# One block of x^T by five transposing transfers of 128 columns instead of one of 640

## The chip, the cores and the metric

The kernel runs on one core of one Trainium2 chip. The metric is the device time of one execution in microseconds; the runs before the change took 182.01, 182.14 and 183.18 us, median 182.14 us. Engine names are those of the profile: PE is TensorE (PEld its weight loads), DVE is VectorE, ACT is ScalarE, POOL is GpSimd, and SP is SyncE, which here only issues DMA transfers (SPq is its queue).

## The reference

Two linear-attention blocks A and B work on the same input x (1 x 2048 x 640, bf16), and a gate made from x mixes their outputs. H is 32, so a head has 20 columns.

```python
def block(x, wqkv, wo):                       # called for A and for B
    qkv = split(x @ wqkv)                     # q, k, v: 32 heads of 20 columns
    phi = lambda t: where(t > 0, t + 1, exp(t)) + 1e-6
    pq, pk = phi(q), phi(k)
    kv = einsum("bhsd,bhse->bhde", pk, v)
    z = pk summed over s
    num = einsum("bhqd,bhde->bhqe", pq, kv)
    den = einsum("bhqd,bhd->bhq", pq, z)[..., None] + 1e-6
    return merge_heads(num / den) @ wo
g = sigmoid((x * gate_w).sum(-1, keepdims=True))
out = g * block(x, A_wqkv, A_wo) + (1 - g) * block(x, B_wqkv, B_wo)
```

## The kernel before

The products x @ wq and x @ wk contract over the 640 columns of x, so TensorE needs x with its columns on the partitions. This is the tile xT, 128 partitions x 5 column groups x 2048 rows: `xT[:, c, s]` holds column 128c + p of row s. A column group c is one step of a contraction; five of them make one product. The rows come in 16 chunks of 128 (D0 to D15 in the plan) and in four blocks of 512.

The first block is filled in two ways: chunks 0 and 1 are transposed by TensorE (`x_transpose`, L290), and rows 256 to 511 by one transposing transfer from DRAM. The second, third and fourth block are each filled by one transposing transfer of 512 rows x 640 columns (L221 and L222), from `load_xT` (L205). All transposing transfers are issued by SP, which works its list strictly in order: first parts of x and of wk of block A, then the half block of xT, then wq of block A in three transfers (L220), then the three blocks of xT, then x in its own layout into the tile xn (L1311 and L1313), then wv (L1230) and wo (L1237, L1240) of block A, and after that wk of block B, which waits for TensorE to be done with wk of block A.

The order of TensorE's, VectorE's and ScalarE's work is written out by hand in the string FIRST (L32 to L50); the engines take the names in that order. For the change this stretch of it matters:

```
... E.P1 ... U0.n0 D2.top D4.c0 D4.c1 E.p1s E.P2 D4.c2 D4.c3 D3.clamp D3.lift0 tq3 sq03 U0.exp0 U0.lift0 tq1
D3.top D3.gl sq01 D4.c4 E.exp0 tq2 D4.exp0 U0.n1 D4.gl sq02 E.clamp D4.clamp D7 ... D6 ... Q00.P5 Q00.P6 ... D5.c0
```

- E.P1 and E.P2 (class `QPair`, L748) are 4 and 6 matmuls of q on block 1 of the rows, 512 columns of output each; E.p1s (L758) is ScalarE's copy of the state between them, so E.P2 waits for that copy. U0.n0 and U0.n1 (class `Fifth`, L388) are 5 matmuls each of the last fifth of q, n0 on the first block of rows, n1 on the second.
- D4 is the first chunk of the second block. D4.c0 to D4.c4 (class `KFirst`, L732, through `k_mm`, L338) are its five column groups, two matmuls of 320 columns each; D4.cN reads column group N of the second block and no other. D5, D6 and D7 are the other chunks of that block, D8 to D11 those of the third, D12 to D15 those of the fourth.
- sq03, sq01, sq02, sq04 (`sq_sum`, L421) are sums and differences of blocks of xT on VectorE. sq03 reads column groups 0 and 1 of the first two blocks, sq01 column groups 0 to 3 of the second.
- tq1 to tq4 (L429) are differences of parts of wq on VectorE, D3.top, D4.clamp, E.clamp and their like VectorE's part of phi, and the names with exp, lift and gl are ScalarE's.

A reader of a tile waits for the transfer that wrote the part it reads. With one transfer for a block, everything that reads any column group of the block waits for the same completion.

Of the kernel before, what the change touches and what calls it, by code (L numbers as in the profile page):

```python
# [9 lines left out]
P = 128  # L10
# [7 lines left out]
DT = D // P  # L18
ST = S // P
NB = 4  # L20
CB = 4
HB = 512
# [56 lines left out]
def kernel(  # L79
# [11 lines left out]
    nc = tc.nc  # L91
    x2 = A_x.flatten_outer_dims()
# [43 lines left out]
    xT = persist.tile([P, DT, S], BF16, name="xT")  # L136
# [62 lines left out]
    def load_x(eng, lo, hi):  # L199
        eng.dma_start(out=xn[:, lo:hi, :], in_=xb0[:, lo:hi, :])  # L200

    def load_wk(eng, lo, hi):
        eng.dma_start(out=wk[0][:, lo:hi, 0:D], in_=wq_dram[0][:, lo:hi, D:2 * D])

    def load_xT(lo, hi):  # L205
        nc.sync.dma_start_transpose(out=xT[:, :, lo:hi], in_=x2[lo:hi, :])

    wq[0] = wpool.tile([P, DT, D], BF16, tag="wq", name="wqA")
    with tc.manual_schedule():
        load_x(nc.sync, 0, 1)  # L210
        load_x(nc.scalar, 1, 2)
        load_wk(nc.sync, 0, 1)
        load_wk(nc.scalar, 1, 2)
        nc.scalar.dma_start(out=g5[:], in_=gate_w.rearrange("(c p) -> c p", p=P))
        load_wk(nc.sync, 2, 3)
        load_wk(nc.sync, 3, DT)
        load_xT(HB // 2, HB)
        nc.scalar.preload_act_table_set("natural_log_exp_and_others")
        for lo, hi in ((0, 2), (2, 4), (4, DT)):
            nc.sync.dma_start(out=wq[0][:, lo:hi, :], in_=wq_dram[0][:, lo:hi, 0:D])  # L220
        for n in range(1, NB):  # L221
            load_xT(n * HB, (n + 1) * HB)  # L222


# [1 line left out]
    for r in range(4):  # L226
# [3 lines left out]
        out=spread[:].rearrange("p (h t) -> p h t", t=TW), in_=I4[:, :, None].to_broadcast([P, H, TW])  # L230
    )
    for lo in range(0, HF, K6):
        part = maskE[:, lo:min(lo + K6, HF)]
        for sign, base in ((1, 0), (-1, Dh - 1)):
            nc.gpsimd.affine_select(
                out=part, in_=part, pattern=[[-sign * Dh, part.shape[1] // Dh], [0, Dh]],
# [3 lines left out]
    for rows, n in ((slice(0, 2 * H), H // 2), (slice(2 * H, P), H)):  # L240
        nc.gpsimd.tensor_copy(
            out=E4_rows[rows, 0:n], in_=I4[rows, 0:n, None].to_broadcast([rows.stop - rows.start, n, Dh])
# [1066 lines left out]
    with tc.manual_schedule():  # L1309
        pts = k_first()  # L1310
        nc.sync.dma_start(out=xn[:, 2:CB, :], in_=xb0[:, 2:CB, :])  # L1311
        for n in range(1, NB):
            nc.sync.dma_start(  # L1313
                out=xn[:, n * CB:(n + 1) * CB, :], in_=x2[n * HB:(n + 1) * HB, :].rearrange("(q p) d -> p q d", p=P)
# [4 lines left out]
        lo, hi = GT  # L1319
# [320 lines left out]
```

## Time and profile before

| | |
|---|---|
| runs, us | 182.01, 182.14, 183.18; median 182.14 |
| the profiled execution's own time, us | 182.23 |
| its span from first to last instruction, us | 180.5 |
| granted TensorE clock | 0.998 |
| DVE busy / ACT busy, us | 151.2 (84%) / 112.4 (62%) |
| DMA packets / MB | 22514 / 19.18 |

A busy share is the time in which an engine works, divided by the span. A row of a timeline gives the start, the duration over the whole group, the engine, the line of the code, the operation, what is written and what is read, and the count; brackets at its end give the idle time of the engine ahead of it and what ended that. A DMA issue's row is the time that the issuing queue spent on it, not the time in which the data moved.

### The profile page before, as it was taken

Reading aid. Unit: us, or ns where it says so; the run is one execution under the profiler, and the core shown is the slowest. Engines: PE = TensorE matmul, PEld = TensorE weight load, DVE = VectorE, ACT = ScalarE, POOL = GpSimd, SP = SyncE. Lnnn points to the kernel's source line nnn. Section 1 sums busy time; section 2 is a strip of 40 time slices with the busy share of each in tenths; the row PEclk is TensorE's granted clock in tenths of the full one; section 3 lists DMA queues with packets and bytes.
Section 4 is the critical chain, followed back from the end, with each engine's and each line's share of the span. In section 5 each row is a group of like instructions: output and inputs, shape, how many; then the busy total and the mean of one; then the engine's idle time right before and its main releaser. Section 6 shows DMA issues by size and latency. Waiting matters only on the chain.

```text
span 180.5 us, 3357 instructions
## 1 busy us (share of the span) xinstructions
PE 176.0 (97%) x1266; PEld 116.8 (65%) x1266; DVE 151.2 (84%) x283; ACT 112.4 (62%) x235; POOL 4.4 (2%) x19
## 2 busy tenths in 40 slices
PE   8989999999999999999999999999999999999993
PEld 3646666665666577566656675766678777777772
DVE  1379999999999996888999997987988979686773
ACT  2387978999763444587778676774715756456410
POOL 7100000000000000000000000000000000000000
PEclk9999999999999999999999999999999999999999
DMA  5999999205046024000000023134902550223133
GB/s 180 309 207 169 237 362 293 66 4 182 0 116 184 5 74 162 0 0 0 2 4 0 2 56 129 44 115 133 252 5 65 150 152 0 84 103 111 73 113 109
DMA packets 22514, 19.18 MB, mean 106 GB/s; under 512 B 10210, under 2 KB 21986, under 8 KB 22498
## 3 DMA queue, kind: packets, MB, share of 16 engines
q1 hardware_dynamic: 21912, 18.47, 37.1%
q10 hardware_dynamic: 586, 0.49, 0.8%
q8 instruction: 10, 0.16, 0.4%
q14 instruction: 6, 0.05, 0.1%
HBM read 11.86 MB, written 4.80 MB: 92 GB/s over the span
## 4 chain that ended last, share of the span: by engine, by line
PE 90%; DMA 4%; SPq 3%; DVE 1%; issue 0%
PE q L522 16%; PE kA L338 9%; PE kB L338 9%; PE gs L840 9%; PE gs L1329 9%; PE oy L1124 6%; PE oz L1124 5%; PE ox L1124 5%; DMA xT<-in_A_x_dram 4%; PE ow L1124 4%; PE kB L522 3%; PE gB L810 2%; PE gA L810 2%; PE qA L388 2%; PE qB L388 1%; PE q L388 1%
## 5 line engine op out<-in xcount | busy, mean ns | idle before, releaser
L338 PEld LDWEIGHTS <-xT 128*128 128x128 bf16 x280 | 27.2, 98 | 15.9 <-DMA xT<-in_A_x_dram 1.1
L338 PE MATMUL kA<-wkA,xT 128*128 128x320 bf16 (+1 forms) x160 | 24.1, 301 | 0.6 <-DMA xT<-in_A_x_dram 0.6
L552 DVE TENSOR_SCALAR e<-e 128x640 bf16<-128x640 bf16 (+2 forms) x59 | 19.1, 334 | 4.6 <-ACT e L546 4.3
L546 ACT ACTIVATE e<-q 128x512 bf16<-128x512 f32 x32 | 18.5, 598 | 5.7 <-PE q L522 5.2
L338 PE MATMUL kB<-wkB,xT 128*128 128x320 bf16 x120 | 19.2, 299 | 0.0
L546 ACT ACTIVATE e<-kB 128x640 bf16<-128x640 f32 (+1 forms) x18 | 11.4, 647 | 7.3 <-PE kB L522 3.2
L546 ACT ACTIVATE e<-kA 128x640 bf16<-128x640 f32 x16 | 11.4, 713 | 4.6 <-PE kA L338 3.9
L528 DVE TENSOR_TENSOR q<-q,p 128x512 f32<-128x512 f32 x16 | 11.1, 695 | 1.7 <-PE q L522 1.2
L559 DVE SCALAR_TENSOR_TENSOR pk<-kB,e 128x640 bf16<-128x640 f32 (+1 forms) x16 | 11.6, 736 | 0.4
L1124 PEld LDWEIGHTS <-xT 128*128 128x128 bf16 x85 | 8.1, 98 | 2.9
L1124 PEld LDWEIGHTS <-pqTA 128*128 128x128 bf16 x85 | 8.1, 98 | 2.8
L1124 PEld LDWEIGHTS <-pqTB 128*128 128x128 bf16 x80 | 7.8, 98 | 3.0
L522 PE MATMUL q<-xT,wqB 128*128 128x512 bf16 x32 | 9.7, 379 | 0.0
L1129 DVE TENSOR_TENSOR osb<-oz,u 128x320 bf16<-128x320 f32 (+2 forms) x18 | 7.9, 452 | 1.9 <-PE oz L1124 1.6
L1187 ACT COPY u<-ox 128x320 f32<-128x320 f32 x8 | 3.4, 426 | 9.4 <-PE ox L1124 9.4
L522 PE MATMUL q<-SQ,TM 128*128 128x512 bf16 x32 | 8.5, 379 | 0.0
L1329 PEld LDWEIGHTS <-xn 128*128 128x128 bf16 x64 | 6.1, 98 | 3.1 <-issue 0.7
L810 PEld LDWEIGHTS <-xn 128*128 128x128 bf16 x64 | 6.3, 98 | 2.8
L840 PEld LDWEIGHTS <-xn 128*128 128x128 bf16 x64 | 6.1, 98 | 2.9 <-issue 0.7
L559 DVE SCALAR_TENSOR_TENSOR pk<-kA,e 128x640 bf16<-128x640 f32 x8 | 6.6, 820 | 0.4
L559 DVE SCALAR_TENSOR_TENSOR pqTB<-q,e 128x512 bf16<-128x512 f32 x10 | 6.8, 683 | 0.0
L1124 PE MATMUL oz<-MB,xT 128*128 128x320 bf16 (+2 forms) x45 | 6.8, 284 | 0.0
(205 smaller groups left out, 373.6 us busy)
## 6 DMA issues: line engine op xcount, KB each, us to landing
out_dram<-osb SPq DMA_DIRECT2D x14, 160.0 KB, 1.8
xn<-in_A_x_dram SPq DMA_DIRECT2D x3, 640.0 KB, 7.8
wvA<-in_A_wqkv_dram SPq DMA_DIRECT2D x1, 800.0 KB, 11.0
wkB<-in_B_wqkv_dram SPq DMA_DIRECT2D x1, 800.0 KB, 4.5
wqB<-in_B_wqkv_dram SPq DMA_DIRECT2D x1, 800.0 KB
wvB<-in_B_wqkv_dram SPq DMA_DIRECT2D x1, 800.0 KB
MA<-m_rows SPq DMA_DIRECT2D x1, 800.0 KB, 4.6
MB<-m_rows SPq DMA_DIRECT2D x2, 400.0 KB, 4.4
```

The lines of the kernel that those rows point to most:

```text
L338: nc.tensor.matmul(pt[:, hf, 0:n], lhsT=xT[:, c, i * P:(i + 1) * P], rhs=wk[b][:, c, hf * HF:hf * HF + n], start=(c == 0), stop=(c == DT - 1),
L388: nc.tensor.matmul(dst, lhsT=mixed(wq[b][:, c, :], m), rhs=xT[:, c, n * HB:(n + 1) * HB], start=first, stop=last,)
L522: nc.tensor.matmul(dst, lhsT=left(c), rhs=right(c), start=first and k == 0, stop=last and k == len(cs) - 1, skip_group_check=not first,)
L528: nc.vector.tensor_tensor(out=dst, in0=acc, in1=sb, op=ALU.add)
L546: nc.scalar.activation(out=self.part(self.e, k), in_=self.srcs[k](), func=ACT.Exp)
L552: nc.vector.tensor_scalar(self.e, self.e, 1.0, EPS, op0=ALU.min, op1=ALU.add)
L559: nc.vector.scalar_tensor_tensor(out=self.part(self.dst, k), in0=src(), scalar=1.0 + EPS, in1=self.part(self.e, k), op0=ALU.add, op1=ALU.max,)
L810: nc.tensor.matmul(pt[:, hf, 0:HF], lhsT=xn[:, i, c * P:(c + 1) * P], rhs=pk[:, i, hf * HF:(hf + 1) * HF], start=(i == 0), stop=(i == ST - 1),
L840: nc.tensor.matmul(pt[:, n, 0:HF], lhsT=left[:, i, n * P:(n + 1) * P], rhs=right[:, i, :], start=(first and i == 0), stop=(i == hc - 1), s ...
L1124: nc.tensor.matmul(dst, lhsT=left[:, c, r0:r0 + P], rhs=right[:, c, :], start=(first and c == 0), stop=(c == DT - 1), skip_group_check=not ...
L1129: nc.vector.tensor_tensor(out=dst, in0=acc, in1=sb, op=ALU.add)
L1329: nc.tensor.matmul(dst[n], lhsT=left[:, i, n * P:(n + 1) * P], rhs=right[:, i, :], start=(first and i == 0), stop=(i == hc - 1), skip_grou ...
```

## The change

`load_xT` gets the column groups as arguments, and the second block of 512 rows is loaded by five transposing transfers of 512 rows x 128 columns, one for each column group in order. The third and the fourth block remain one transfer of 512 x 640 each. All are issued by SP at the same place in its list as before.

```diff
-    def load_xT(lo, hi):
-        nc.sync.dma_start_transpose(out=xT[:, :, lo:hi], in_=x2[lo:hi, :])
+    def load_xT(lo, hi, c0=0, c1=DT):
+        nc.sync.dma_start_transpose(out=xT[:, c0:c1, lo:hi], in_=x2[lo:hi, c0 * P:c1 * P])
...
-        for n in range(1, NB):
+        for c in range(DT):
+            load_xT(HB, 2 * HB, c, c + 1)
+        for n in range(2, NB):
             load_xT(n * HB, (n + 1) * HB)
```

P is 128, DT is 5, HB is 512 and NB is 4.

## The prediction

> **What bounds the kernel now.** I read the page's busy line and the shares of the chain that ended last first.
>
> ```profile
> PE 176.0 (97%) x1266; PEld 116.8 (65%) x1266; DVE 151.2 (84%) x283; ACT 112.4 (62%) x235; POOL 4.4 (2%) x19
> ...
> PE 90%; DMA 4%; SPq 3%; DVE 1%; issue 0%
> ```
>
> PE is busy in all but 180.5 - 176.0 = 4.5 us of the span, and the chain is PE nearly throughout. A change to a load can save no more than those 4.5 us, and only the part of them that a load causes. The list of PE's waits over the whole span has two rows:
>
> ```profile
> PE warm L252 <- PEq L1624: 0.8, 1, 0.8
> PE kA L338 <- DMA xT<-in_A_x_dram: 0.6, 1, 0.6
> ```
>
> The first is the start of the program. The second is the only time in the run that matmuls wait for data by this view, and it is for xT. The chain of waits, asked for the first 20 us, shows the place:
>
> ```profile
> 5.87 0.04 issue
> 5.91 7.59 DMA xT<-in_A_x_dram
> 13.51 0.05 issue
> 13.55 0.72 PE kA L338 x4
> 14.27 1.29 PE qA L748 x6
> 15.57 0.82 PE kA L338 x6
> ```
>
> The transfer that SP began to issue at 5.91 is the second block. It landed 7.59 us later, at 13.50, and from there the chain is PE to the very end but for 1% of DVE. So what is saved at 13.55 can reach the end. The timeline gives the engines around it:
>
> ```profile
> 10.81 1.02 PE L748 MATMUL qA<-xT,wqA 128*128 128x512 bf16 x4
> ...
> 11.68 1.24 PE L388 MATMUL qA<-xT,wqA 128*128 128x512 bf16 x5
> ...
> 11.99 0.75 DVE L429 TENSOR_TENSOR MB<-wqA 128x512 bf16<-128x512 bf16 x1
> ...
> 13.53 0.69 DVE L421 TENSOR_TENSOR SQ<-xT 128x1024 bf16<-128x1024 bf16 x1 [0.79 <-DMA xT<-in_A_x_dram]
> 13.55 0.39 PEld L338 LDWEIGHTS <-xT 128*128 128x128 bf16 x4 [1.11 <-DMA xT<-in_A_x_dram]
> 13.55 0.72 PE L338 MATMUL kA<-wkA,xT 128*128 128x320 bf16 x4 [0.63 <-DMA xT<-in_A_x_dram]
> ...
> 14.11 1.46 PE L748 MATMUL qA<-xT,wqA 128*128 128x512 bf16 x6
> ...
> 14.34 0.20 ACT L719 ACTIVATE gl<-kA 128x1 f32<-128x1 f32 x1
> ...
> 15.61 1.02 ACT L546 ACTIVATE e<-qA 128x1024 bf16<-128x1024 f32 x1 [1.07 <-PE qA L748]
> ```
>
> U0.n0 (the x5 at 11.68) is followed by D4.c0 and D4.c1 (the x4 at 13.55), then E.P2 (14.11). D4.c0 and c1 need column groups 0 and 1 only, sq03 on DVE (13.53) as well, yet all three engines stand: PE 0.63 us, PEld 1.11, DVE 0.79, and ACT 1.07 because E.P2 is late.
>
> **How much the wait is worth.** Matmul starts are the safest clock, since ends are modelled. Four matmuls of 512 columns take 11.68 - 10.81 = 0.87 us, 0.217 each. Five from 11.68 end their turn at 11.68 + 5 x 0.217 = 12.76: there D4.c0 would start. It started at 13.55, so the wait costs 0.79 us. After it the pitch is normal (four matmuls in 14.11 - 13.55 = 0.56 us, 0.14 each), so nothing more is lost by restarting.
>
> **When the pieces land.** The rates of the DMA engines in the stretches before the landing:
>
> ```profile
> 10.00:10.50 0.50, 0.50 (x6) 0.38 (x4) 0.13 (x1) 0.50 (x3) 0.00 (x0) 1.00 1.13 253
> 10.50:11.00 0.50, 0.50 (x5) 0.33 (x4) 0.50 (x2) 0.50 (x1) 0.00 (x0) 1.00 1.28 290
> 11.00:11.50 0.50, 0.50 (x4) 0.25 (x3) 0.50 (x2) 0.49 (x1) 0.00 (x0) 1.00 1.27 289
> 11.50:12.00 0.50, 0.50 (x4) 0.33 (x3) 0.50 (x3) 0.34 (x2) 0.00 (x0) 1.00 1.05 233
> 12.00:12.50 0.50, 0.50 (x4) 0.24 (x3) 0.50 (x2) 0.50 (x1) 0.00 (x0) 1.00 0.49 114
> 12.50:13.00 0.50, 0.42 (x2) 0.00 (x0) 0.24 (x1) 0.50 (x2) 0.00 (x0) 1.00 1.13 104
> 13.00:13.50 0.50, 0.00 (x0) 0.00 (x0) 0.00 (x0) 0.50 (x2) 0.00 (x0) 1.00 0.85 130
> ```
>
> The last number is GB/s, so half of it is the KB of a stretch: 126, 145, 144, 116, 57, 52 and 65, in all 705 KB. The block is 512 x 640 x 2 bytes = 655 KB, a piece 131 KB. Suppose the block's bytes were the very last that moved before 13.50, the latest reading. Then they began 50 KB after 10.00, near 10.2, and in order the five pieces are complete when 181, 312, 443, 574 and 705 KB have moved: at 10.7, 11.1, 11.6, 12.4 and 13.5 us. D4.c0 needs its piece at 12.76 and D4.c1 at 12.76 + 2 x 0.14 = 13.04, so both have some 2 us to spare for being announced. c2 is due after the four matmuls and E.P2's six: 12.76 + 0.56 + 6 x 0.217 = 14.62, c3 at 14.90, c4 at 15.18, all beyond the 13.5 of the whole block. sq03 could start when tq3 ends, at 11.99 + 0.75 = 12.74. So the wait of 0.79 us goes, and nothing in the data's order puts another in its place. If one reads the block as ending earlier and the low rates after 12.0 as a pause, the first pieces only come earlier.
>
> **What five transfers cost.** SP's rows:
>
> ```profile
> 2.67 1.55 SPq L206 DMA_TRANSPOSE xT<-in_A_x_dram x1
> ...
> 5.91 12.39 SPq L206 DMA_TRANSPOSE xT<-in_A_x_dram x3
> 18.35 0.58 SPq L1311 DMA_DIRECT2D xn<-in_A_x_dram  x1
> 18.98 1.57 SPq L1313 DMA_DIRECT2D xn<-in_A_x_dram  x3
> 20.59 0.52 SPq L1230 DMA_DIRECT2D wvA<-in_A_wqkv_dram  x1
> ```
>
> No transfer of 512 x 128 is in this trace. The nearest is the half block of 256 x 640, 1.55 us to issue. If issue goes with the amount, a piece (131 of 328 KB) is 0.62 us and five are 3.1, no more than the 12.39 / 3 = 4.1 us of one block now; it may even be less, but data that wait behind wq gain nothing by that. If it is all fixed, five are 7.75 us: they would be issued at 7.5, 9.1, 10.6, 12.2 and 13.7, and SP would be some 3.6 us late afterwards. I take the amount, because a block of twice the rows took more than twice as long. At the dear end c4 matters: after 13.7 it must still land. The nearest transfer of that size alone is a store:
>
> ```profile
> out_dram<-osb SPq DMA_DIRECT2D x14, 160.0 KB, 1.8
> xn<-in_A_x_dram SPq DMA_DIRECT2D x3, 640.0 KB, 7.8
> wvA<-in_A_wqkv_dram SPq DMA_DIRECT2D x1, 800.0 KB, 11.0
> ```
>
> With 1.8 us c4 lands at 15.5, 0.3 after it is due: a gain of 0.5 instead of 0.8.
>
> **What is queued behind on SP.** The third block, the fourth, xn, wv and wo would be late by up to those 3.6 us. Their first readers:
>
> ```profile
> 22.71 1.53 PE L338 MATMUL kA<-wkA,xT 128*128 128x320 bf16 x10
> ...
> 29.19 1.52 PE L338 MATMUL kA<-wkA,xT 128*128 128x320 bf16 x10
> ```
>
> ```profile
> 35.62 0.68 DVE L1060 TENSOR_TENSOR S<-xn 128x1024 bf16<-128x1024 bf16 x1
> ```
>
> ```profile
> DMA to landing us min/median/max: 6.6/7.1/7.6
> ```
>
> ```profile
> SPq L1230 <- PE kA L338: 14.9, 1, 14.9
> ```
>
> D9 at 22.71 reads the third block first, D15 at 29.19 the fourth. The last issue of a block ends at 18.30, and issue to landing is at most 7.6 us by the row of all transposes; even an issue begun at 18.30 would land at 25.9, ahead of D15, and the third block's issue lies a whole block's issue (4.1 us) earlier than the fourth's, which began no later than 18.3 - 4.1 = 14.2: so the third began near 10.1 and landed by 17.7. That is 5.0 us ahead of D9, or 4.2 when D9 itself comes 0.79 sooner: 3.6 us fit. xn is issued by 20.55 and lands in 7.8, at 28.4, against 35.62. wv and wo have no reader there, and SP then waits 14.9 us for PE before its next transfer. So the extra issue costs nothing even at the dear end.
>
> **Does the gain reach the end?** PE's next work has to be fed by engines that move up as well. DVE has no gap of its own from 13.53 on:
>
> ```profile
> 14.00:15.00 1.00, 1.00 (x7) 0.59 (x6) 1.00 (x3) 0.54 (x2) 0.00 (x0) 1.00 1.28 291
> ```
>
> But its 0.79 us of idle time ends with the same landing, so its string starts at 12.74 instead of 13.53. ACT ends its earlier work at 14.34 + 0.20 = 14.54 and would get E.P2's result at 15.61 - 0.79 = 14.82: still in time. All three shift by 0.79 us, and what they wait for among themselves shifts with them. Sum for the profiled execution: 182.23 - 0.79 = 181.44 us. It lies 0.09 above the median of 182.14, so the median would be 181.35; I say 181.4.
>
> **Rivals.** *The gain is lost in part or whole (2 in 10).* A pause like the one that the rates show after 12.0 (114, 104, 130 GB/s against 290) falls on the first pieces instead, or DVE's or ACT's string, with a quarter of a microsecond to spare on ACT, becomes late next. For it: DVE is at 1.00 there. Against it: three engines were freed by one landing. Price: anything between 0 and 0.6 of the 0.79 remaining, 181.6 to 182.2. Here belongs also the case that it does not do what it says: that the transfer's completion was not the issue but the DMA engines were, so that c0 and c1 also land near 13.5, which is 182.1.
>
> *Slower: the pieces run one after the other (6 in 100).* If a transposing transfer starts only when the one before it has been acknowledged, the round trip of 1.8 us that a lone 160 KB transfer shows is paid per piece. With c0 at 11.2 (10.7 and half a microsecond), c1 lands at 13.0, c2 at 14.8, c3 at 16.6 and c4 at 18.4. D4.c4 started at 14.11 + 6 x 0.217 + 4 x 0.14 = 15.97 in the run before, so the end is 2.4 us later: 184.6. It decides from a pitch of (15.97 - 11.2) / 4 = 1.2 us per piece. Against it: rates of 290 GB/s at 14.0 to 15.0 right after the landing at 13.5, with the next block already issued, show transfers flowing without such a gap; at 266 GB/s, the mean of 10 to 12, a piece's data take 0.5 us. The Trainium skill, DMA: Bandwidth & Descriptors, section Rules for kernel authors, speaks against the change: many small transfers should be coalesced into a large one. Its section Anatomy of one DMA puts the fixed cost near 2.0 us per DMA (for another kind of issue); paid in series with 0.3 us of data this estimate would be 2.3 us per piece, c4 at 20.4 and a time of 186.6; no row shows that it adds up for transfers in one queue.
>
> *Slightly slower (5 in 100)*: a fixed cost of 1.2 to 1.4 us per piece, up to 0.8 us slower, to 182.9. *Faster than the forecast (4 in 100)*: the most that any row holds for PEld's wait is 1.11 us, 181.0; beyond this only a cause that I do not see.
>
> **How the numbers follow.** The forecast has 65 in 100, its own range 181.1 to 181.7. The range 180.9 to 182.5 takes in PEld's bound below and the lost gain above with the 0.1 to 0.3 us by which runs differ, and leaves out the series and most of the rest, below 2 in 10. A measurement of this kernel tells about 1%, 1.8 us, from no change. The forecast and the lost gain are within it, 85 in 100; of the slower cases the series (6) and a tail (3) are beyond it, of the faster ones 3: faster 0.03, same 0.88, slower 0.09.
>
> **What would show it.** Right: no wait of PE or DVE for xT near 13, D4's first matmuls at about 12.8, E.P2's at 13.3, D4.c4 near 15.2, five transposes on SP in 3 to 5 us, and a span near 179.7. Wrong: a wait of PE for xT at D4.c2, c3 or c4 (pieces too slow), D4.c0 still near 13.5 (the engines, not the completion), or D9 waiting (SP late). If D4.c0 is early and the span is still 180.5, a later wait took the gain back.

## The result and the profile after

The changed kernel took 181.26 us (median of 7 runs, 180.88 to 181.48), the kernel before 182.38 us (7 runs, 182.01 to 183.18). The ratio is 0.9934, 95% interval 0.9913 to 0.9956: 1.1 us less. The profiled execution took 180.88 us, its span is 179.2 us.

The page of the changed kernel, engine sums and the chain that ended last:

```profile
PE 175.1 (98%) x1266; PEld 116.2 (65%) x1266; DVE 151.1 (84%) x283; ACT 112.4 (63%) x235; POOL 4.4 (2%) x19
...
PE 95%; DMA 2%; DVE 1%; ACTq 0%; issue 0%
```

The share of DMA in the chain fell from 4% to 2%, and what is left of it is another transfer (the gate's weights, at the very start). PE's waits over the whole span of the changed kernel:

```profile
PE warm L254 <- PEq L1626: 0.8, 1, 0.8
PE warm L268 <- DMA g<-in_gate_w_dram: 0.4, 1, 0.4
```

The wait for xT is not among them. The timeline of the changed kernel at the place where PE, DVE and ACT stood before (start, duration, what):

```profile
10.53 1.03 PE L750 MATMUL qA<-xT,wqA 128*128 128x512 bf16 x4
...
11.39 1.24 PE L390 MATMUL qA<-xT,wqA 128*128 128x512 bf16 x5
...
12.36 0.70 DVE L423 TENSOR_TENSOR SQ<-xT 128x1024 bf16<-128x1024 bf16 x1
12.47 0.71 PE L340 MATMUL kA<-wkA,xT 128*128 128x320 bf16 x4
...
13.03 1.46 PE L750 MATMUL qA<-xT,wqA 128*128 128x512 bf16 x6
...
14.32 0.99 PE L340 MATMUL kA<-wkA,xT 128*128 128x320 bf16 x6
14.52 1.02 ACT L548 ACTIVATE e<-qA 128x1024 bf16<-128x1024 f32 x1 [0.26 <-PE qA L750]
```

D4.c0 starts at 12.47 = 11.39 + 5 x 0.217, without a bracket; sq03 on DVE starts at 12.36 as soon as its engine is free. E.P1 began at 10.53 here and at 10.81 before, so 0.28 us of the lead over the first profile existed ahead of the change's place: D4.c0 leads by 13.55 - 12.47 = 1.08, of which 0.80 is the wait. The lead stays. PE's last group of matmuls, before and after:

```profile
176.60 0.85 PE L1124 MATMUL oz<-MB,xT 128*128 128x192 bf16 x10
```

```profile
175.52 0.85 PE L1126 MATMUL oz<-MB,xT 128*128 128x192 bf16 x10
```

These are 1.08 us apart, but the two executions differ by 182.23 - 180.88 = 1.35 us. The other 0.26 or so lie behind the last matmuls: the span ends 3.91 us after the start of that group before and 3.65 after. There SP waits for the counters by which the transfers announce their landing, one wait after the other (five of these seven rows; the first starts at 179.4 before and at 177.1 after):

```profile
L1635 SPq EVENT_SEMAPHORE  x7: 17/28/28, 179.4 to 180.5; - x7
```

```profile
L1637 SPq EVENT_SEMAPHORE  x7: 17/28/28, 177.1 to 179.1; - x7
```

The trace's records show how this hangs on the number of transfers. Eight counters are given to the transfers in turn, and SP's five closing waits ask for them in a fixed order. Before, the last store (the writing of the last result) has a counter of the first wait: all five end after it has landed, 0.06 to 0.07 us apart. With four transfers more it has a counter of the fifth, and the other four waits are over when it lands. The store itself lands 2.8 us after the start of the last group in both.

SP's list in the changed kernel:

```profile
6.22 13.03 SPq L206 DMA_TRANSPOSE xT<-in_A_x_dram  x7
19.30 0.58 SPq L1313 DMA_DIRECT2D xn<-in_A_x_dram  x1
```

and its transposing transfers one by one (shortest, median and longest issue in ns):

```profile
L206 SPq DMA_TRANSPOSE xT<-in_A_x_dram x8: 1153/1262/3579, 2.7 to 15.7; - x8
```

Five transfers of 131 KB cost SP 1.15 to 1.26 us each. That is twice the 0.62 us that the prediction took; all five need 6.4 us, where it expected 3 to 5. And xn is issued 0.95 us later than before (19.30 against 18.35).

### The profile page after: what moved, and what is told of

Its sections match the earlier page's. It is cut to its first block, busy times and chain, and to the rows that moved or that the text cites. A ratio compares the mean times of both kernels' runs of the same rounds, so it can differ in the third digit from the quotient of the medians.

```text
span 179.2 us, 3362 instructions
## 1 busy us (share of the span) xinstructions
PE 175.1 (98%) x1266; PEld 116.2 (65%) x1266; DVE 151.1 (84%) x283; ACT 112.4 (63%) x235; POOL 4.4 (2%) x19
## 4 chain that ended last, share of the span: by engine, by line
PE 95%; DMA 2%; DVE 1%; ACTq 0%; issue 0%
PE q L524 16%; PE kA L340 12%; PE kB L340 9%; PE gs L842 9%; PE gs L1331 9%; PE oy L1126 6%; PE oz L1126 5%; PE ox L1126 5%; PE ow L1126 4%; PE kB L524 3%; PE gB L812 2%; PE gA L812 2%; PE qA L390 2%; DMA g<-in_gate_w_dram 2%; PE q L390 1%; PE qA L750 1%
## 5 line engine op out<-in xcount | busy, mean ns | idle before, releaser
L548 ACT ACTIVATE e<-kA 128x640 bf16<-128x640 f32 x16 | 11.3, 712 | 4.5 <-PE kA L340 3.8
```

The costliest lines, as they stand in the source:

```text
L548: nc.scalar.activation(out=self.part(self.e, k), in_=self.srcs[k](), func=ACT.Exp)
```

## The experiments

Theory 1: the gain is the wait for the completion of a whole block, of which only column groups 0 and 1 are needed at first. Rivals: more and smaller transfers move the block sooner, whatever waits for them; PE's wait alone counts, without DVE; the start of the run is the source of a part. Ratios are to the kernel before, run beside each.

**The change once more.**

> The changed kernel once more, with its own profile. Theory 1 (a wait for the completion of a whole block was removed, worth 0.8 us, and the further 0.3 us of the first comparison come from the first loads of the run, which land by chance a few tenths earlier or later): D4's first matmul starts 0.55 us after the last of U0.n0's five starts by the normal pitch, no PE wait for the second block; ratio to the kernel before between 0.993 and 0.997. Theory 2 (the change also makes the start of the run faster): E.P1 starts near 10.5 again, not 10.8, and the ratio is again near 0.993.

Measured: 181.45 us (180.98 to 182.11), ratio 0.9947 (0.9922 to 0.9971). The time agrees, and E.P1 was early again (10.40), as theory 2 said; on this see below. The profile brought something else. PE ran from U0.n0 into D4.c0 without a wait (12.34 = 11.26 + 5 x 0.217), but the last piece was late. PE's timeline and the chain of waits of that run:

```profile
14.18 0.71 PE L340 MATMUL kA<-wkA,xT 128*128 128x320 bf16 x4
15.92 0.45 PE L340 MATMUL kA<-wkA,xT 128*128 128x320 bf16 x2 [1.02 <-DMA xT<-in_A_x_dram]
```

```profile
9.92 1.26 SPq L206
11.18 0.04 issue
11.22 4.66 DMA xT<-in_A_x_dram
15.88 0.04 issue
15.92 0.45 PE kA L340 x2
```

The fifth piece was issued from 11.22 on, because the four ahead of it kept SP 1.2 to 1.3 us each, and landed at 15.88, 1.1 us after D4.c4 was due (14.18 + 4 x 0.14 = 14.74). In this execution the gain at the load was given back: PE's last group starts at 176.58, against 176.60 in the first profile of the kernel before.

**Two pieces.**

```diff
-        for c in range(DT):
-            load_xT(HB, 2 * HB, c, c + 1)
+        for c0, c1 in ((0, 2), (2, DT)):
+            load_xT(HB, 2 * HB, c0, c1)
```

> Second block by two transfers, column groups 0 and 1, then 2 to 4. Theory 1 (only the completion that c0, c1 and sq03 wait for matters): the first piece lands near 12.0, where c1 landed with five, no PE wait, ratio as with five (0.993 to 0.996). Theory 2 (it is the small size of the pieces that brings the data sooner): the first piece lands later than 12.8, a part of the PE wait of 0.6 us is back, ratio 0.996 to 1.000.

Measured: 181.23 us (181.16 to 181.70), ratio 0.9951 (0.9931 to 0.9970). PE's chain runs through the place with no piece of DMA between U0.n0 (the x5), D4.c0 and c1 (x4), E.P2 (x6) and the rest:

```profile
11.97 1.08 PE qA L390 x5
13.05 0.55 PE kA L340 x4
13.60 1.29 PE qA L750 x6
14.89 0.82 PE kA L340 x6
15.72 1.08 PE qA L390 x5
```

By the trace's completion records the piece with c0 and c1 lands at 11.5 us (column group 1 of the five lands at 12.1, 11.3 and 11.7 in the three profiles of the change). That is not later than 12.8, so theory 2 falls. Five are not needed: what counts is that c0 and c1 are announced apart from the rest.

**The same five in reverse order.**

```diff
-        for c in range(DT):
+        for c in reversed(range(DT)):
```

> The same five transfers in the order 4, 3, 2, 1, 0. Theory 1 (what counts is when column groups 0 and 1 are announced): c0 lands last, near 14.1, D4.c0 starts there, PE waits some 1.3 us and the time is 0.4 to 0.6 us above the kernel before, ratio 1.002 to 1.004. Theory 2 (five transfers move the block faster, or help elsewhere, whatever their order): ratio 0.993 to 0.996 as with the change.

Measured: 185.21 us (183.53 to 186.59), ratio 1.0151 (1.0109 to 1.0192). The same bytes in the same number of transfers are 2.8 us slower than the kernel before, so theory 2 falls. Theory 1 has the sign, but the size is several times what it said. PE's wait is 2.2 us, and after it PE is slow:

```profile
14.86 0.76 PE L340 MATMUL kA<-wkA,xT 128*128 128x320 bf16 x4 [2.24 <-DMA xT<-in_A_x_dram]
15.43 2.76 PE L750 MATMUL qA<-xT,wqA 128*128 128x512 bf16 x6
```

E.P2's six matmuls take 2.76 us instead of 1.46. The windows of the same run show why (the number ahead of the last two is the granted clock):

```profile
14.00:15.00 1.00, 0.14 (x1) 0.11 (x2) 0.09 (x1) 0.24 (x2) 0.00 (x0) 1.00 0.91 155
15.00:16.00 1.00, 1.00 (x6) 0.60 (x5) 1.00 (x2) 0.00 (x0) 0.00 (x0) 0.71 1.25 276
16.00:17.00 1.00, 1.00 (x4) 0.29 (x2) 1.00 (x3) 0.00 (x0) 0.00 (x0) 0.50 1.03 227
17.00:18.00 1.00, 1.00 (x4) 0.31 (x3) 1.00 (x3) 0.00 (x0) 0.00 (x0) 0.50 1.91 120
18.00:19.00 1.00, 1.00 (x6) 0.61 (x5) 0.48 (x1) 0.78 (x1) 0.00 (x0) 0.58 0.26 44
```

The granted clock falls to 0.50. The share of 0.71 between 15 and 16 us puts the fall at 15.4, half a microsecond after PE had started again, and the shares of 0.71, 0.50, 0.50 and 0.58 make 3.4 us at half speed. The Trainium skill, TensorE: Matmul & The Clock Gate, section Part 1: The HAM clock gate, says that the clock is halved after an idle window of about 3.4 us. Here it fell after 2.24 us of idle PE, while 1.02 us (the change's second profile) and 1.85 us (the run by rows, below) left it at 1.00.

By starts, PE lost 2.4 us at the wait (14.86 against 11.38 + 1.08), 1.6 more than in the kernel before, and another 1.7 us in the slow stretch behind it (its last group follows D4.c0 by 164.73 us here, by 163.05 before). The other executions agree: the one of the six whose clock stayed at 1.00 took 183.53 us, the five others, at 0.989 to 0.991, took 184.97 or more.

**Four pieces by rows.** D4 reads only the first 128 rows of the block, sq03 all of them.

```diff
-        for c in range(DT):
-            load_xT(HB, 2 * HB, c, c + 1)
+        for q in range(CB):
+            load_xT(HB + q * P, HB + (q + 1) * P)
```

> Second block by four transfers of 128 rows x 640 columns: D4 needs the first alone, sq03 on DVE needs all four. PE's D4.c0 is then free near 12.5, DVE's sq03 only when the block is complete, 13.5 to 14.1. Theory A (the gain needs DVE to move up with PE, as the prediction argued): PE runs on at once but waits for DVE within the next 10 us, and the ratio is 0.998 to 1.004. Theory B (PE's own wait is all that counts, DVE has slack): the gain of 0.8 us stays, ratio 0.993 to 0.996.

Measured: 183.12 us (182.34 to 184.08), ratio 1.0040 (1.0014 to 1.0066). Theory A holds. PE went from U0.n0 into D4.c0 at once, but its next wait was for DVE, and the chain of waits of this run leads from the load through DVE and ACT back to PE:

```profile
10.62 4.45 DMA xT<-in_A_x_dram
...
15.29 0.10 DVE SQ L423
...
19.36 1.23 DVE pqTA L561
...
20.67 0.59 ACT q L776
...
21.96 0.60 ACT pk L551
22.56 0.04 issue
22.60 1.54 PE kA L340 x10
```

The block was complete at 15.07, sq03 started at 15.29 instead of 13.53, 1.76 us later, and PE was later by about the same: D5's matmuls, which started at 20.90 before, start at 22.60, 1.70 us later, and PE's last group at 178.31 instead of 176.60. This block landed 1.6 us later than in the first profile of the kernel before (13.50), so the run frees PE and delays DVE at once; the next one leaves the load as it is.

**PE's order changed, loads as before.**

```diff
-U0.n0 D2.top D4.c0 D4.c1 E.p1s E.P2 D4.c2 D4.c3
+U0.n0 D2.top E.p1s E.P2 D4.c0 D4.c1 D4.c2 D4.c3
```

> The kernel before, its loads untouched; only PE's order is changed: E.P2 ahead of D4.c0 and D4.c1, so that PE has work of 1.3 us while the second block lands. Theory A (DVE has to move up too; in the kernel before DVE's sq03 waits for the same landing, and the slack between its later pk and the q matmul that waited for it in the run by rows was 0.4 us): PE's wait goes, but only about 0.4 us of it reach the end, ratio 0.997 to 0.999. Theory B (PE's wait alone counts): 0.65 us, since E.P2 starts only when its copy is done at 12.9, ratio 0.995 to 0.997.

Measured: 182.74 us (182.19 to 183.57), ratio 1.0015 (1.0001 to 1.0030). PE filled its wait and nothing came of it, less than even theory A said. The chain of waits has the same form:

```profile
6.20 7.76 DMA xT<-in_A_x_dram
13.96 0.02 issue
13.98 0.04 DVE SQ L421
...
21.30 1.54 PE kA L338 x10
```

sq03 starts at 13.98, 0.45 us later than in the first profile because this execution's block landed that much later, and D5's matmuls start at 21.30, 0.40 later. In both runs PE follows DVE's start to within 0.1 us. The expected slack of 0.4 us was read at q's matmuls. D5's matmuls behind them wait for ACT's pk, the end of the same string (0.21 us in both runs), and there none was left.

**All three blocks by five.**

```diff
-        for c in range(DT):
-            load_xT(HB, 2 * HB, c, c + 1)
-        for n in range(2, NB):
-            load_xT(n * HB, (n + 1) * HB)
+        for n in range(1, NB):
+            for c in range(DT):
+                load_xT(n * HB, (n + 1) * HB, c, c + 1)
```

> Second, third and fourth block by five transfers each, 15 in all. Theory 1 (each transfer of 512 x 128 keeps SP 1.3 us whatever its size): SP issues the last near 26, the fourth block lands near 27, just ahead of sq13 and D15 near 28, and x in its own layout, issued until 28, lands near 36, after its first reader on DVE at 34.5: time 0 to 2 us above the change, ratio to the kernel before 0.995 to 1.008. Theory 2 (issue goes with the amount, 0.6 us): SP is no later than with the change, ratio 0.993 to 0.997.

Measured: 181.48 us (181.24 to 181.73), ratio 0.9942 (0.9927 to 0.9958). SP's rows:

```profile
6.20 20.55 SPq L206 DMA_TRANSPOSE xT<-in_A_x_dram  x15
26.79 0.58 SPq L1312 DMA_DIRECT2D xn<-in_A_x_dram  x1
```

Fifteen transfers kept SP 20.55 us, 1.37 each, and xn was issued 8.4 us later than in the kernel before, yet PE has no wait for data and DVE none for xn. Theory 1 has the time on SP, the last issue ending near 26.8. Its ratio, 0.995 or more, was missed: it reckoned with delays that did not come. So xn's issue has at least 8 us of slack here, and the added issue of the change costs nothing there.

**Ten pieces.**

```diff
         for c in range(DT):
-            load_xT(HB, 2 * HB, c, c + 1)
+            for r in range(2):
+                load_xT(HB + r * HB // 2, HB + (r + 1) * HB // 2, c, c + 1)
```

> Second block by ten transfers of 256 rows x 128 columns, column group by column group. Theory 1 (a fixed time of 1.2 to 1.3 us on SP per transfer): the ten need 12 to 13 us to issue, c1 is complete near 12.5, c2 near 15, c4 near 20; PE waits 3 to 5 us for c2, c3 and c4, ratio 1.015 to 1.035. Theory 2 (issue goes with the amount): the ten need 6.5 us, ratio as with the change.

Measured: 187.03 us (186.85 and 187.21), ratio 1.0246 (1.0224 to 1.0269). Transfers of half the size cost SP the same:

```profile
L206 SPq DMA_TRANSPOSE xT<-in_A_x_dram x13: 1240/1241/3624, 2.7 to 22.4; - x13
```

PE waits 0.68 us at D4.c3 and 2.19 us at D4.c4, and the granted clock is 0.50 to 0.66 from 20 to 24 us. Theory 1 holds, with waits of 2.9 us, just under the 3 to 5 that it expected: the time on SP is per transfer, not per byte, between 66 and 131 KB.

**More profiles of the changed kernel, the kernel before and two pieces.**

> The changed kernel, one more profile, to see how steady the last piece's landing is. It landed at 14.1 in the first profile and at 15.9 in the second, with D4.c4 due at 14.9 and 14.7. Theory 1 (c4 has about 0.8 us to spare and a pause of the DMA engines takes it in some executions): it lands between 14.0 and 16.0, and PE's wait for it is between 0 and 1 us. Theory 2 (the second profile was a single event): it lands near 14.1 and PE does not wait.

Measured: 181.05 us, no wait of PE for xT after the first half block. With the runs above, the fifth piece of the block came late in one of four profiles (the first, this one and the run with all blocks by five show none). It landed at 14.0 here, which both theories allow.

> The kernel before, one more profile, to see how long its wait for the second block is from one execution to the next. The four comparisons of kernels that removed it gave 0.9934 to 0.9951, about 1.0 us on the mean, against 0.8 us for the wait in the first profile. Theory 1 (the landing of the whole block varies with pauses of the DMA engines, and 0.8 us was a short wait): PE waits 0.6 to 1.6 us at D4.c0. Theory 2 (the wait is steady and the rest lies elsewhere, in the start or the end of the run): 0.6 to 0.7 us by the list of waits, as in the first profile.

> As the look before: theory 1 expects a wait at D4.c0 between 0.6 and 1.6 us that differs from look to look, theory 2 the same 0.6 to 0.7 us.

> As the two looks before: theory 1 expects a wait at D4.c0 between 0.6 and 1.6 us that differs from look to look, theory 2 the same 0.6 to 0.7 us.

Measured: 182.30, 182.72 and 182.51 us. The wait at D4.c0, by starts as in the prediction, is 0.81 us (13.63 against 11.74 + 1.08), 1.02 (13.95 against 11.85 + 1.08) and 1.25 (13.84 against 11.51 + 1.08). The row and the chain of the third of them:

```profile
13.84 0.72 PE L338 MATMUL kA<-wkA,xT 128*128 128x320 bf16 x4 [1.09 <-DMA xT<-in_A_x_dram]
```

```profile
5.87 7.92 DMA xT<-in_A_x_dram
13.80 0.05 issue
13.84 0.72 PE kA L338 x4
```

Theory 1 holds for the wait, which differs: the first profile's, 0.79, was the shortest of the four. Theory 2 has a part too, for the end of the program adds its 0.26 us.

> Two pieces once more, to see whether the second piece (column groups 2 to 4, due near 14.7) is as steady as the first profile's 13.4. If the issue time per transfer is what makes the last of five late (issued by 12.5 with five, by 10.7 with two), it lands between 12.5 and 14.5 and PE does not wait; if pauses of the DMA engines alone decide, it can be as late as 15.9, as with five, and PE waits up to 1 us.

Measured: 181.49 us, no wait of PE for the second block. In both profiles of two pieces the block is complete ahead of its need: the transfers' completion records put the second piece at 13.5 and 13.6 us, those of five pieces put the fifth at 14.1, 15.9, 14.0 and 14.3. Two profiles are too few to exclude a late one.

## Why the prediction was right, and where it was off

*The wait.* Right in place, and in size for the execution from which it was worked out: 0.79 us forecast, 0.80 us gone between the two profiles. The measured gain is larger, 1.1 us between the medians, and the forecast held two of its parts too small. The wait itself was taken from one profile: four give 0.79, 0.81, 1.02 and 1.25, mean 0.97. And the end of the program was taken as fixed, where 0.26 us went, a by-product of the number of transfers and not of the load. It shows in all profiles: from the start of PE's last group to the end of the span there are 3.90 to 3.91 us in the kernel before (four profiles) and with PE's order changed, 3.65 with four transfers more (three profiles of the change, and the reversed run) and with twelve more, 3.69 with three more, 3.82 to 3.84 with one more and with nine more. One and nine agree, and four and twelve, as they must with eight counters in turn.

With both, the profiles account for the medians. In nine profiles (the four before, the two of the change without a late piece, both of two pieces and all blocks by five) PE's last group follows D4.c0 by 163.04 to 163.06 us, so D4.c0's start tells the end. It is 13.74 on the mean of the four profiles before, and 12.88 on the mean of the three of the change (12.47, 12.65, and 13.53 for the one with the late piece, counted back from its last group), 0.86 us sooner: 0.97 for the wait and 0.29 for an earlier U0.n0, less 0.40 for the late piece. With the 0.26 us this makes 1.12. That it is the measured gain to the digit is luck, with so few profiles.

The kernel before stood at an absolute time, the block's landing (13.50 to 13.96 in five profiles of its loads), however early PE got there; with the wait gone, what the start of a run wins or loses passes through to the end. How early a run gets there was not settled: E.P1 started at 10.40, 10.53 and 10.70 us in the three profiles of the change, at 10.65 to 10.98 in the four of the kernel before, at 10.95 and 10.96 with two pieces and at 11.38 with all blocks by five. The loads ahead of it are the same in all, so chance is one reading, but the change's three are on the early side and 0.2 to 0.3 us of its gain may lie there. The four ratios of kernels that announce c0 and c1 early are 0.9934, 0.9947, 0.9951 and 0.9942, mean 0.9944, which is 1.0 us of 182.4.

That 181.4 lies so near 181.26 is in part luck: the forecast starts from a median of three runs, 182.14, and that of seven was 182.38.

*Only the announcement of column groups 0 and 1.* Right: two pieces gain as much as five, within the intervals of the ratios, and the reverse order of the same five costs 2.8 us, some 1.7 of it by the clock.

*DVE has to move up too.* Right. Where PE alone was freed (the run by rows, PE's order), PE came back to DVE's string within 8 us, and its last group started as late as sq03 had started late, to within 0.1 us.

*Cost of five transfers.* The step that failed: "I take the amount, because a block of twice the rows took more than twice as long", 0.62 us each. Measured are 1.15 to 1.26 us for 131 KB and 1.24 for 66 KB, near the other bound (1.55 us, all fixed). The row that misled was a block's 4.1 us. In these runs a block of 512 x 640 took SP 2.9 to 5.1 us, also 4.4 us for the one issued at 13.9, when wq had landed (10.3 us by the records); what sets it was not settled, and it does not scale down to a piece. By the measured times the fifth piece is issued from 11.3 on and not from 8.7, and the 1.7 us that the prediction saw between its landing and D4.c4 shrank to 0.8 in the first profile, and to less than none in one of four. The time from issue to landing, 1.8 us after a store, was short as well: the fifth piece took 2.8 to 2.9 us from the beginning of its issue in three profiles and 4.66 in the fourth. The forecast survived because its bound had been reckoned through: 0.5 of the 0.8 us would have been left.

*SP behind the change.* Right: nothing waits, and with another 7.5 us of delay of xn nothing waited either.

*The rivals.* The series of pieces, each waiting for the last to be acknowledged, did not come: issues follow one another at 1.3 us, whatever has landed. But this pitch is beyond the 1.2 us from which that rival would have decided, and it lies in the range of the rival "slightly slower". What decides is the pitch of the landings. By the records they are 11.60, 12.08, 12.56, 13.32 and 14.12 us in the first profile, 0.63 apart on the mean, because issuing began at 6.2 us and had done four pieces before the first landed. In the second profile they are 10.77, 11.26, 12.36, 13.57 and 15.88, 1.28 apart, and there the gain at the load was gone. So the pitch that the series needs was reached in one profile of four, without its mechanism, and it cost the gain and no more.

The Trainium skill's advice to coalesce (DMA: Bandwidth & Descriptors, section Rules for kernel authors), named in the prediction, holds here only down to two pieces: two have the gain of five, with the last piece 0.4 us or more earlier, and ten cost 2.5%, but a single transfer is 0.5% behind two.

## What to carry to other kernels

When several engines wait for one large transfer and need only its first part, split it so that this part has its own completion, in the order of need, and no further: each transposing transfer held the issuing queue for 1.2 us or more even at 66 KB. Before filling one engine's wait by reordering, see who else waits for the same event; the gain is what the last of them gains. And take the size of a wait from several profiles, for a transfer's landing moved by half a microsecond between executions here while the work ahead of it moved on its own. Last, a change in the number of transfers can shift the end of the program by itself, here by up to 0.26 us: compare the time behind the last matmul before crediting all of a small gain to the load.

## What the runs showed of the hardware

- The issue of a transposing transfer took SP 1.24 us for 256 rows x 128 columns (66 KB) and 1.26 for 512 x 128 (131 KB): half the bytes saved nothing.
- The granted clock fell to 0.50 behind 2.24 and 2.19 us of idle PE, in both cases after PE had started again, and stayed there for 3.4 us (by the shares of the windows); after 1.02 and 1.85 us it did not fall. What decides between them was not settled.
- A piece of 131 KB took 4.66 us from the beginning of its issue to its landing in one profile (the chain of the second profile), the same piece 2.8 to 2.9 in three others. What held it there was not settled: no run here takes that apart.
- At the end of this program SP's waits for the counters of the transfers follow one another at 0.06 to 0.07 us. Which of the five is the last store's moves the end of the span by up to 0.26 us, from 3.91 to 3.65 us behind the start of the last matmuls.
